# Cross network on one core: weight loads in another order and on other queues, the last tiles in another order, the last group's sums and stores moved

## The chip, the cores and the metric

The kernel runs on one core of a Trainium2 chip. The metric is device microseconds (us) of one execution, the median over several. The core has five engines, each with its own instruction queue in program order: PE (TensorE, matmuls), DVE (VectorE), ACT (ScalarE), POOL (GpSimd) and SP (SyncE), which here only issues DMAs. ACT can issue DMAs too, on a queue of its own. Engines and DMAs wait for each other by semaphores.

## The reference

A deep-and-cross network: six layers, each a 416 x 416 projection of x with a bias, multiplied element by element by x0 and added to x.

```python
B, F, D, L = 16384, 26, 16, 6
Din = min(F * D, 1024)          # 416
...
x = x0
for l in range(L):
    proj = jnp.einsum('bd,de->be', x, ws[l]) + bs[l]
    x = x0 * proj + x
return x
```

All inputs and the output are bf16.

## The kernel before

**Layout.** The 16384 rows are cut into 8 groups of 2048 rows. A group is held transposed (features on partitions, rows along the free dimension), in 4 chunks of 512 rows (`j`, 0 to 3). The 416 features are three blocks of 128 (`t` or `i`, 0 to 2) and a tail of 32. The tails of the four chunks lie under each other on 128 partitions (`x3s`, and the last 512 columns of `x0s`). The weights of a layer are `wm[l]` (the first 384 input features), `w3[l]` (the last 32, repeated four times under each other, one copy for each chunk) and `wbd[l]` (the 32 x 32 corner, block-diagonal, which POOL copies out of `w3` in `make_wbd`).

**Tiles.** A tile (g, l, i) is output block i of layer l of group g: 12 matmuls of 128 x 512 (`full`, L402) and 4 that use 32 rows of the array, side by side (`rows32`, L414), into four PSUM banks. ACT adds the bias and moves the tile to SBUF (`evacuate`, L361), DVE multiplies by x0 (L370) and adds x (L375). The tails of several jobs are computed together (`tails`, L427 and L432, then L388, L390, L392). Mostly two tiles are paired: the first runs `full` and then `rows32`, the second `rows32` and then `full`.

**Order.** A list `order` walks the 48 jobs (g, l) along diagonals, so that several groups are in flight and PE does not wait for the job before it. In that list the tile (6, 5, 2), the third block of the last layer of group 6, is taken out and put at the end (L550, L551), behind the three tiles of (7, 4). Job (7, 5), the last layer of the last group, is not in the list; it is done by the code from L657 on. For job (7, 4) and for (0, 0) the third block is evacuated chunk by chunk (`fine_after`, `step = 1`).

**A small scheduler.** Every instruction is recorded with `add`, with the names it reads and writes. `Program` derives the waits and writes out one queue for each engine. Each queue keeps the order of the `add` calls, but for DVE: an instruction with `hold` is put behind the next one with `release`, so that the sum of a piece stands after the product of the next piece. A DMA belongs to a `lane`, a semaphore of its own; a reader of one DMA of a batch waits for the whole batch of its lane. At the end SP waits for every lane (L162, L179).

**The start.** Group 0 is loaded row-major in four pieces of 512 rows (L457, SP's queue, 416 KB each) and transposed by PE (`transposed_chunk`, L483 and L488; ACT evacuates blocks 0 and 1, L493, DVE the rest, L496 and L499). Twenty-eight matmuls on the identity (L469) come first. The biases (L459) and layer 0's weights (`load_w(0, "act")`, L279 and L281) go over ACT's queue, layer 1's over SP's. PE then does chunk 0, the biases, chunk 1, the first three matmuls of tile (0, 0, 0), chunk 2, three more, chunk 3, and the rest. The other groups are loaded by transposing DMAs on SP (`load_group`, L295 to L302), with the weights of later layers among them (`W_LOAD`).

**The output of groups 0 to 6** (`output`, L520): three transposing DMAs for the three blocks (L524), four for the tails (L529), into one staging tile `ost`, and one store of 1664 KB (L535), all on SP. It is recorded once a group's last tile and its tails are done.

**The last stage, job (7, 5)**, is computed row-major, so that its output needs no transpose. The rows of each chunk are taken in four residues, blocks `kk` of 0 to 3. For each kk and chunk j, `nat_full` (L700) and `nat_rows` (L711, L716) make the projection with the bias; `nat_mul` copies it to SBUF on ACT (L728) and multiplies by x0 on DVE (L730; the very last directly from PSUM, L725); `nat_add` adds x (L735). `to_rows` turns x of two blocks at a time to row-major on PE (L675, L682), evacuated half by ACT (L692), half by DVE (L695). `nat_store` (L740) stores a block of 416 KB, the last one in two halves. Four banks `bka` and four banks `bkb` are used in turn.

Of the kernel before, what the change touches and what calls it, by code (L numbers as in the profile page):

```python
# [3 lines left out]
P = 128  # L4
CH = 512
T32 = 32
# [15 lines left out]
class Program:  # L22
# [125 lines left out]
    def emit(self):  # L148
        nc = self.nc
        self.flush()  # L150
        self._solve()
        sems = {e: nc.alloc_semaphore(f"sem_{e}") for e in self.ENGINES if e != "sp"}
        for lane in self.lanes:
            sems[lane] = nc.alloc_semaphore(f"sem_{lane}")
        count = {}
        for e, ops in self.queue.items():
            n = 0
            for op in ops:
                if op.need and op.lane is None:
                    n += 1  # L160
                count[id(op)] = n
        ends = [(lane, 16 * sum(len(ops) for _, ops in b)) for lane, b in self.lanes.items()]  # L162

        def run(e, handle):
            for op in self.queue[e]:
                for dom, val, d in op.waits:
                    handle.wait_ge(sems[dom], val if d.lane is not None else count[id(d)])
                ins = op.fn(handle)
                if op.lane is not None:
                    ins.then_inc(sems[op.lane], 16)  # L170
                elif op.need:
                    ins.then_inc(sems[e], 1)

        with nc.Block("main") as block:

            @block.sync
            def _(h):
                run("sp", h)
                for lane, n in ends:  # L179
                    h.wait_ge(sems[lane], n)  # L180

            @block.gpsimd
            def _(h):
                run("pool", h)

            @block.scalar
            def _(h):
                run("act", h)

            @block.tensor  # L190
            def _(h):
                run("pe", h)

            @block.vector
            def _(h):
                run("dve", h)


def bass_standalone__cross_network_dcn__recsys_kernel(
# [75 lines left out]
        return got  # L275


    def load_w(l, eng):
        add(eng, lambda h: h.dma_start(wm[l][:, :, :], ws[l, 0:NT * P, :].rearrange("(t p) f -> p t f", p=P)),  # L279
            writes=[("wm", l)], lane=f"w{l}", batch=0)  # L280
        add(eng, lambda h: h.dma_start(w3[l][:, :], ws[l, NT * P:D, :].unsqueeze(0).broadcast_to([NJ, T32, D])),  # L281
            writes=[("w3", l)], lane=f"w{l}", batch=0)

    def make_wbd(l):
        add("pool", lambda h: h.memset(wbd[l][:, :], 0.0), writes=[("wbd", l)])
        for j in range(NJ):
            q = slice(j * T32, (j + 1) * T32)
            add("pool", lambda h, q=q: h.tensor_copy(wbd[l][q, q], w3[l][q, NT * P:D]),  # L288
                reads=[("w3", l)], writes=[("wbd", l)])

    def load_group(g):
        s = slot(g)
# [116 lines left out]
    def rows32(g, l, i, banks, first):  # L409
        src, stok = x3_src(g, l)  # L410
        ecols = slice(i * P, (i + 1) * P)
        for j in range(NJ):
            q = slice(j * T32, (j + 1) * T32)
            add("pe", lambda h, q=q, j=j: h.matmul(  # L414
                bank(banks[j]), w3[l][q, ecols], src[q, :], start=first, stop=not first,
                tile_position=(j * T32, 0)),
                reads=stok + [("w3", l)], writes=[("ps", banks[j])])

    def tails(batch):
        bs_ = take(len(batch))  # L420
# [32 lines left out]
        return ap[j * CH:(j + 1) * CH, :].rearrange("(p k) f -> p k f", k=KK)  # L453

    g0 = x0[0:GC, :]
    for j in range(NJ):
        add("sp", lambda h, j=j: h.dma_start(x0n[:, j, :, :], perm(g0, j)),  # L457
            writes=[("nat", j)], lane=f"nat{j}", batch=0)
    add("act", lambda h: h.dma_start(bs_sb[0:L, :], bs[:, :]), writes=["bs_sb"], lane="bs", batch=0)  # L459
    load_w(0, "act")  # L460
    make_wbd(0)
    load_w(1, "sp")
    load_group(1)
    load_w(2, "sp")
    make_wbd(1)
    make_wbd(2)

# [7 lines left out]
    def transposed_chunk(j):  # L475
        ba, bb = (0, 1) if j % 2 == 0 else (2, 3)
        s = slot(0)
        for t in range(NT + 1):
            b, o = (ba, t * CH) if t < 2 else (bb, (t - 2) * CH)
            for k in range(KK):  # L480
                c = slice(o + k * P, o + (k + 1) * P)
                if t < NT:
                    add("pe", lambda h, t=t, k=k, b=b, c=c: h.transpose(  # L483
                        psum_t(b)[:, c], x0n[:, j, k, t * P:(t + 1) * P], ident[:, :]),
                        reads=[("nat", j), x0_tok(nat, 0, 0), "ident"], writes=[("ps", b)])
                else:
                    q = slice(j * T32, (j + 1) * T32)
                    add("pe", lambda h, k=k, b=b, c=c, q=q: h.matmul(  # L488
                        psum_t(b)[q, c], x0n[:, j, k, NT * P:D], ident[:, :], is_transpose=True,
                        tile_position=(0, j * T32)),  # L490
                        reads=[("nat", j), x0_tok(nat, 0, 0), "ident"], writes=[("ps", b)])
        for t in range(2):
            add("act", lambda h, t=t: h.activation(  # L493
                x0s[s][:, cols(t, j)], psum_t(ba)[:, t * CH:(t + 1) * CH], ACT_F.Copy),
                reads=[("ps", ba)], writes=[x0_tok(s, t, j)])
        add("dve", lambda h: h.tensor_copy(x0s[s][:, cols(2, j)], psum_t(bb)[:, 0:CH]),  # L496
            reads=[("ps", bb)], writes=[x0_tok(s, 2, j)])
        q = slice(j * T32, (j + 1) * T32)
        add("dve", lambda h: h.tensor_copy(x0s[s][q, XW:XW + CH], psum_t(bb)[q, CH:2 * CH]),  # L499
            reads=[("ps", bb)], writes=[("x03q", s, j)])  # L500
# [19 lines left out]
    def output(g):  # L520

        s, s3 = xset[(g, L)], xtail[(g, L)]
        for t in range(NT):
            add("sp", lambda h, t=t: h.dma_start_transpose(  # L524
                ost[:, :, t * P:(t + 1) * P], xs[s][:, t * GC:(t + 1) * GC]),
                reads=[("x", s, t, j) for j in range(NJ)], writes=[("ost", t)], lane="ot", batch=g)
        for j in range(NJ):
            q = slice(j * T32, (j + 1) * T32)
            add("sp", lambda h, j=j, q=q: h.dma_start_transpose(  # L529
                ost[:, j * KK:(j + 1) * KK, NT * P:D], x3s[s3][q, :]),  # L530
                reads=[("x3", s3)], writes=[("ost", NT, j)], lane="ot", batch=g)
        rows = out[g * GC:(g + 1) * GC, :]
        pat = "(j p k) f -> p j k f" if g == 0 else "(j k p) f -> p j k f"
        kw = dict(j=NJ, k=KK)
        add("sp", lambda h: h.dma_start(  # L535
            rows.rearrange(pat, **kw), ost[:, :, :].rearrange("p (j k) f -> p j k f", j=NJ)),
            reads=[("ost", t) for t in range(NT)] + [("ost", NT, j) for j in range(NJ)],
            writes=[("out", g)], lane="out", batch=g)
        free_x.append(s)
        free_3.append(s3)  # L540
# [7 lines left out]
            if (jb, i) in where:  # L548
                items.append(("tails", where[(jb, i)]))
    late = items.index(("tile", (LAST - 1, L - 1), NT - 1))  # L550
    items.append(items.pop(late))  # L551


    single = 0
# [18 lines left out]
    def start_job(g, l):  # L573
        started.add((g, l))
        xset[(g, l + 1)] = free_x.pop(0)
        if (g, l) in W_LOAD:
            load_w(W_LOAD[(g, l)], "sp")
            make_wbd(W_LOAD[(g, l)])
        if (g, l) in G_LOAD:
            load_group(G_LOAD[(g, l)])  # L580
# [124 lines left out]
    def nat_rows(kk, bks, first):  # L705
        for part in range(2):
            for j in range(NJ):
                q = slice(j * T32, (j + 1) * T32)
                st, sp_ = first and part == 0, not first and part == 1
                if part == 0:  # L710
                    add("pe", lambda h, j=j, q=q, st=st: h.matmul(  # L711
                        bank(bks[j], n=D), x3col(j, kk), w3[l][q, :], start=st, stop=False,
                        tile_position=(j * T32, 0)),
                        reads=tok3 + [("w3", l)], writes=[("ps", bks[j])])
                else:
                    add("pe", lambda h, j=j, sp_=sp_: h.matmul(  # L716
                        bank(bks[j], n=D), ones[j * T32:j * T32 + 1, :], brow[j * T32:j * T32 + 1, :],
# [17 lines left out]
        add("dve", lambda h: h.tensor_tensor(o, o, x5v, ALU.add),  # L735
            reads=[("on", j, kk), ("x5n", j, kk // 2)], writes=[("on", j, kk)])

    def nat_store(kk, j0, j1, lane):
        dst = out[LAST * GC:B, :].rearrange("(j p k) f -> p j k f", j=NJ, k=KK)[:, j0:j1, kk, :]
        add("sp", lambda h: h.dma_start(dst, on[:, j0:j1, kk, :]),  # L740
            reads=[("on", j, kk) for j in range(j0, j1)], writes=[("out7", kk, j0)], lane=lane, batch=0)

    bka, bkb = take(NJ), take(NJ)
# [6 lines left out]
    for j in range(NJ):  # L750
        nat_full(1, j, bkb[j], False)
        nat_mul(1, j, bkb[j])
    to_rows(0, bka)
    for kk in range(2):
        for j in range(NJ):
            nat_add(kk, j)
        nat_store(kk, 0, NJ, f"o7_{kk}")
    nat_rows(2, bkb, True)
    for j in range(NJ):
        nat_full(2, j, bkb[j], False)  # L760
        nat_mul(2, j, bkb[j])
    to_rows(1, bka)
    for j in range(NJ):
        nat_add(2, j)
    nat_store(2, 0, NJ, "o7_2")
    nat_rows(3, bkb, True)
    for j in range(NJ):
        nat_full(3, j, bkb[j], False)
        nat_mul(3, j, bkb[j])
        nat_add(3, j)  # L770
        if j % 2 == 1:
            nat_store(3, j - 1, j + 1, f"o7_3_{j}")

    pr.emit()

# [27 lines left out]
```

## Time and profile before

| what | value |
|---|---|
| median of 6 runs | 498.66 us (497.05 to 500.68) |
| the profiled execution | 498.28 us, of which 496.5 us are its span |
| PE busy | 478.5 us (96%) |
| DVE busy | 405.5 us (82%) |
| ACT busy | 342.7 us (69%) |
| POOL busy | 9.5 us (2%) |
| mean granted clock of PE | 0.989 |
| DMA | 47.65 MB, mean 96 GB/s |

The span runs from the first to the last instruction. Where a time is given without more, it is counted from the span's start. In the profile, a line of an engine's timeline has the start, the duration over all its instructions, the engine, the line of the kernel, the operation with what it writes and reads, how many, and in brackets the idle time before it and what ended it. SPq and ACTq are DMA issues on these queues. The granted clock is the share of full speed that PE was given.

The largest waits of the profile, in all:

| who waited | for | us |
|---|---|---|
| ACT, L361 | PE, L414 | 106.6 |
| DVE, L370 | ACT, L361 | 68.1 |
| POOL, L288 | DMA of the weights | 39.8 |
| ACT, L361 | PE, L402 | 23.5 |
| DVE, L496 | PE, L488 | 12.8 |
| PE, L402 | DMA of the weights | 3.0 |

### The profile page before, as it was taken

Reading aid. Unit: us, or ns where it says so; the run is one execution under the profiler, and the core shown is the slowest. Engines: PE = TensorE matmul, PEld = TensorE weight load, DVE = VectorE, ACT = ScalarE, POOL = GpSimd, SP = SyncE. Lnnn points to the kernel's source line nnn. Section 1 sums busy time; section 2 is a strip of 40 time slices with the busy share of each in tenths; the row PEclk is TensorE's granted clock in tenths of the full one; section 3 lists DMA queues with packets and bytes.
Section 4 is the critical chain, followed back from the end, with each engine's and each line's share of the span. In section 5 each row is a group of like instructions: output and inputs, shape, how many; then the busy total and the mean of one; then the engine's idle time right before and its main releaser. Section 6 shows DMA issues by size and latency. Waiting matters only on the chain.

```text
span 496.5 us, 8094 instructions
## 1 busy us (share of the span) xinstructions
PE 478.5 (96%) x3251; PEld 203.2 (41%) x3251; DVE 405.5 (82%) x710; ACT 342.7 (69%) x371; POOL 9.5 (2%) x37
## 2 busy tenths in 40 slices
PE   6999999999999999999999999999999999999990
PEld 5433444444444444434444444444444444444460
DVE  1578888888888888888888888888888888888892
ACT  3667767677677777667677767767667767777680
POOL 2002100000000000000000000000000000000000
PEclk9999999999999999999999999999999999999997
DMA  9797880000001694347516944560000452334428
GB/s 247 148 197 138 154 179 5 1 1 0 2 1 26 111 241 80 50 87 193 129 33 106 245 73 72 130 214 1 1 1 1 79 106 93 61 76 141 85 55 275
DMA packets 127185, 47.65 MB, mean 96 GB/s; under 512 B 107298, under 2 KB 125612, under 8 KB 127148
## 3 DMA queue, kind: packets, MB, share of 16 engines
q1 hardware_dynamic: 126604, 46.71, 42.8%
q8 instruction: 25, 0.41, 0.4%
q10 hardware_dynamic: 544, 0.43, 0.3%
q14 instruction: 12, 0.10, 0.1%
HBM read 5.97 MB, written 13.63 MB: 39 GB/s over the span
## 4 chain that ended last, share of the span: by engine, by line
PE 92%; DVE 3%; DMA 2%; ACT 1%; issue 0%; ACTq 0%
PE ps L402 74%; PE ps L414 8%; PE ps L427 6%; PE ps L432 2%; DMA w<-in_ws_dram 2%; DVE x L735 1%; PE ps L700 1%; DVE x L375 1%; ACT tw L361 1%; DVE tw L370 1%; PE ps L483 0%; DVE x L695 0%; DVE x L730 0%; PE ps L675 0%; PE ps L488 0%
## 5 line engine op out<-in xcount | busy, mean ns | idle before, releaser
L361 ACT ACTIVATE tw<-ps,bias 128x1024 bf16<-128x1024 f32 (+1 forms) x295 | 300.4, 1073 | 130.0 <-PE ps L414 106.6
L402 PE MATMUL ps<-x,wm 128*128 128x512 bf16 x1692 | 380.5, 380 | 3.9 <-DMA w<-in_ws_dram 3.0
L370 DVE TENSOR_TENSOR tw<-tw,x 128x1024 bf16<-128x1024 bf16 (+1 forms) x286 | 194.2, 683 | 68.7 <-ACT tw L361 68.1
L402 PEld LDWEIGHTS ps<-x,wm 128*128 128x128 bf16 x1692 | 159.0, 98 | 218.8 <-issue 31.6
L375 DVE TENSOR_TENSOR x<-tw,x 128x1024 bf16<-128x1024 bf16 (+1 forms) x286 | 182.0, 677 | 0.0
L414 PE MATMUL ps<-x,w 32*128 32x512 bf16 x564 | 44.5, 380 | 0.4 <-DVE x L392 0.4
L427 PE MATMUL ps<-x,wm 128*32 128x512 bf16 x564 | 38.7, 380 | 0.0
L388 ACT ACTIVATE ts<-ps,bias 128x512 bf16<-128x512 f32 x47 | 28.7, 699 | 0.0
L414 PEld LDWEIGHTS ps<-x,w 32*128 32x128 bf16 x564 | 9.0, 92 | 33.5 <-issue 32.4
L427 PEld LDWEIGHTS ps<-x,wm 128*32 128x32 bf16 x564 | 13.8, 96 | 15.5 <-issue 3.2
L392 DVE TENSOR_TENSOR x<-ts,x 128x512 bf16<-128x512 bf16 x47 | 18.6, 417 | 0.0
L390 DVE TENSOR_TENSOR ts<-ts,x 128x512 bf16<-128x512 bf16 x47 | 18.5, 417 | 0.0
L432 PE MATMUL ps<-x,wbd 128*32 128x512 bf16 x188 | 18.3, 379 | 0.0
L496 DVE COPY x<-ps 128x512 bf16<-128x512 bf16 x4 | 1.7, 424 | 12.8 <-PE ps L488 12.8
L493 ACT ACTIVATE x<-ps 128x512 bf16<-128x512 bf16 x8 | 4.3, 594 | 7.5 <-PE ps L483 7.5
L700 PE MATMUL ps<-wm,x 128*128 128x416 bf16 x48 | 9.2, 341 | 0.0
L288 POOL COPY wbd<-w 32x32 bf16<-32x32 bf16 x24 | 7.4, 307 | 41.0 <-DMA w<-in_ws_dram 39.8
L432 PEld LDWEIGHTS ps<-x,wbd 128*32 128x32 bf16 x188 | 5.0, 97 | 5.1
L728 ACT ACTIVATE x<-ps 128x416 bf16<-128x416 f32 x15 | 6.5, 545 | 0.5 <-PE ps L716 0.5
L700 PEld LDWEIGHTS ps<-wm,x 128*128 128x128 bf16 x48 | 5.1, 115 | 3.8 <-issue 1.3
L735 DVE TENSOR_TENSOR x<-x,x 128x416 bf16<-128x416 bf16 x16 | 5.1, 371 | 0.1
L730 DVE TENSOR_TENSOR x<-x,x 128x416 bf16<-128x416 bf16 x15 | 4.8, 369 | 0.0
(32 smaller groups left out, 38.9 us busy)
## 6 DMA issues: line engine op xcount, KB each, us to landing
out_dram<-ost SPq DMA_DIRECT2D x7, 1664.0 KB, 6.8
x<-in_x_dram SPq DMA_DIRECT2D x8, 416.0 KB, 6.4
wm<-in_ws_dram SPq DMA_DIRECT2D x5, 312.0 KB
out_dram<-x SPq DMA_DIRECT2D x3, 416.0 KB, 6.9
x<-Tb SPq DMA_DIRECT2D x28, 32.0 KB, 1.9
ost<-x SPq DMA_TRANSPOSE x49, 3.0
w<-in_ws_dram SPq DMA_DIRECT2D x5, 104.0 KB
out_dram<-x SPq DMA_DIRECT2D x2, 208.0 KB, 5.7
```

The costliest lines, as they stand in the source:

```text
L361: add("act", lambda h, a=a, w=w, b0=b0: h.activation(tw[r][:, a * CH:(a + w) * CH], psum[:, b0 * CH:(b0 + w) * CH], ACT_F.Identity, bias=b ...
L370: add("dve", lambda h, a=a, e=e: h.tensor_tensor(tw[r][:, a * CH:e * CH], tw[r][:, a * CH:e * CH], x0s[s0][:, i * GC + a * CH:i * GC + e * ...
L375: add("dve", lambda h, a=a, e=e: h.tensor_tensor(xs[so][:, i * GC + a * CH:i * GC + e * CH], tw[r][:, a * CH:e * CH], src(i, a, e), ALU.ad ...
L388: add("act", lambda h: h.activation(ts[r][:, :], bank(b), ACT_F.Identity, bias=bias[:, 3, l:l + 1], scale=1.0), reads=[("ps", b), "bias"], ...
L390: add("dve", lambda h: h.tensor_tensor(ts[r][:, :], ts[r][:, :], x0s[s0][:, XW:XW + CH], ALU.mult), reads=[("ts", r)] + x03_toks(s0), writ ...
L392: add("dve", lambda h: h.tensor_tensor(x3s[so][:, :], ts[r][:, :], src, ALU.add), reads=[("ts", r)] + stok, writes=[("x3", so)], hold=True)
L402: add("pe", lambda h, t=t, j=j: h.matmul(bank(banks[j]), wm[l][:, t, ecols], src(t, j, j + 1), start=(first and t == 0), stop=(not first a ...
L414: add("pe", lambda h, q=q, j=j: h.matmul(bank(banks[j]), w3[l][q, ecols], src[q, :], start=first, stop=not first, tile_position=(j * T32, 0)),
L427: add("pe", lambda h, t=t, j=j, src=src, l=l, b=b: h.matmul(bank(b, j * T32, (j + 1) * T32), wm[l][:, t, NT * P:D], src(t, j, j + 1), star ...
L432: add("pe", lambda h, j=j, s3=s3, l=l, b=b: h.matmul(bank(b, j * T32, (j + 1) * T32), wbd[l][:, j * T32:(j + 1) * T32], s3, start=False, s ...
L700: add("pe", lambda h, t=t: h.matmul(bank(b, n=D), xcol(t, j, kk), wm[l][:, t, :], start=(first and t == 0), stop=(not first and t == NT - 1)),
L735: add("dve", lambda h: h.tensor_tensor(o, o, x5v, ALU.add), reads=[("on", j, kk), ("x5n", j, kk // 2)], writes=[("on", j, kk)])
```

## The change

1. **Weights.** `load_w` becomes `load_wm` and `load_w3`, each with a lane of its own. `w3` is loaded by four DMAs of 32 rows instead of one that repeats the rows; its readers depend on their copy (one lane, so they wait for all four).
2. **Load order at the start.** The first row-major piece is loaded in two halves (two of its four row residues each), each with its lane. Layer 0's `wm` follows on SP's queue, then the other three pieces, then layer 1's `wm`. The `w3` of layers 0 and 1 go over ACT's queue, eight DMAs behind the biases. From layer 2 on both parts are on SP's.
3. **Output of groups 0 to 6.** The transposing DMA of block 2 comes after those of the tails.
4. **Tile order.** (6, 5, 2) is put before the last tile instead of behind it: (7, 4, 1), (6, 5, 2), (7, 4, 2). With that (7, 4, 2), which was the second of a pair with its chunks evacuated between its matmuls, stands alone: all its matmuls, `rows32`, then the four evacuations.
5. **Last stage.** The second `to_rows` goes to before the sums of blocks 0 and 1, with banks `bkb`; block 2 takes `bka`, its `nat_rows` before those sums. In blocks 2 and 3 each sum comes one product later. The last half of the last store is issued on ACT's queue.
6. **End.** SP waits for the lanes of the output only.

```diff
-        ends = [(lane, 16 * sum(len(ops) for _, ops in b)) for lane, b in self.lanes.items()]
+        ends = [(lane, 16 * sum(len(ops) for _, ops in b)) for lane, b in self.lanes.items() if lane.startswith("out")]
...
-    def load_w(l, eng):
+    def load_wm(l, eng):
         add(eng, lambda h: h.dma_start(wm[l][:, :, :], ws[l, 0:NT * P, :].rearrange("(t p) f -> p t f", p=P)),
-            writes=[("wm", l)], lane=f"w{l}", batch=0)
-        add(eng, lambda h: h.dma_start(w3[l][:, :], ws[l, NT * P:D, :].unsqueeze(0).broadcast_to([NJ, T32, D])),
-            writes=[("w3", l)], lane=f"w{l}", batch=0)
+            writes=[("wm", l)], lane=f"wm{l}", batch=0)
+
+    def load_w3(l, eng):
+        for j in range(NJ):
+            add(eng, lambda h, j=j: h.dma_start(w3[l][j * T32:(j + 1) * T32, :], ws[l, NT * P:D, :]),
+                writes=[("w3", l, j)], lane=f"w3{l}", batch=0)
...
-    for j in range(NJ):
-        add("sp", lambda h, j=j: h.dma_start(x0n[:, j, :, :], perm(g0, j)),
-            writes=[("nat", j)], lane=f"nat{j}", batch=0)
+    def load_nat(j, k0, k1):
+        add("sp", lambda h: h.dma_start(x0n[:, j, k0:k1, :], perm(g0, j)[:, k0:k1, :]),
+            writes=[("nat", j, k) for k in range(k0, k1)], lane=f"nat{j}{k0}", batch=0)
+
     add("act", lambda h: h.dma_start(bs_sb[0:L, :], bs[:, :]), writes=["bs_sb"], lane="bs", batch=0)
-    load_w(0, "act")
+    load_nat(0, 0, 2)
+    load_nat(0, 2, KK)
+    load_wm(0, "sp")
+    load_w3(0, "act")
     make_wbd(0)
-    load_w(1, "sp")
+    for j in range(1, NJ):
+        load_nat(j, 0, KK)
+    load_wm(1, "sp")
+    load_w3(1, "act")
     load_group(1)
-    load_w(2, "sp")
+    load_wm(2, "sp")
+    load_w3(2, "sp")
...
-        for t in range(NT):
-            add("sp", lambda h, t=t: h.dma_start_transpose(
+        def turn(t):
+            add("sp", lambda h: h.dma_start_transpose(
...
+        turn(0)
+        turn(1)
         for j in range(NJ):
...
+        turn(2)
...
-    items.append(items.pop(late))
+    items.insert(len(items) - 2, items.pop(late))
...
-    def nat_store(kk, j0, j1, lane):
+    def nat_store(kk, j0, j1, lane, eng="sp"):
...
     to_rows(0, bka)
+    to_rows(1, bkb)
+    nat_rows(2, bka, True)
     for kk in range(2):
         for j in range(NJ):
             nat_add(kk, j)
-        nat_store(kk, 0, NJ, f"o7_{kk}")
-    nat_rows(2, bkb, True)
+        nat_store(kk, 0, NJ, f"out7_{kk}")
     for j in range(NJ):
-        nat_full(2, j, bkb[j], False)
-        nat_mul(2, j, bkb[j])
-    to_rows(1, bka)
-    for j in range(NJ):
-        nat_add(2, j)
-    nat_store(2, 0, NJ, "o7_2")
+        nat_full(2, j, bka[j], False)
+        nat_mul(2, j, bka[j])
+        if j:
+            nat_add(2, j - 1)
+    nat_add(2, NJ - 1)
+    nat_store(2, 0, NJ, "out7_2")
     nat_rows(3, bkb, True)
     for j in range(NJ):
         nat_full(3, j, bkb[j], False)
         nat_mul(3, j, bkb[j])
-        nat_add(3, j)
-        if j % 2 == 1:
-            nat_store(3, j - 1, j + 1, f"o7_3_{j}")
+        if j:
+            nat_add(3, j - 1)
+        if j == 2:
+            nat_store(3, 0, 2, "out7_3")
+    nat_add(3, NJ - 1)
+    nat_store(3, 2, NJ, "out7_4", "act")
```

## The prediction

> **What bounds the kernel now.** I read the busy shares first: TensorE (PE) is busy 478.5 of 496.5 us, so only about 18 us can be won without removing matmuls. The waits say where they lie: 1.8 us before the identity exists, 3.0 us for the first weights, about 1 us at 25 us; the rest, 12 us, is the stretch after PE's last matmul (484.5 us). The middle is a solid PE stream that the change does not touch. So I read two timelines, the first 17 us and the last 40. The head (start, duration, engine, line):
>
> ```profile
> 1.36 0.41 ACTq L279 DMA_DIRECT2D wm<-in_ws_dram  x1
> 1.80 0.65 ACTq L281 DMA_DIRECT2D w<-in_ws_dram  x1
> 2.48 1.28 ACT L493 ACT_TABLE_LOAD   x1 [2.48 <-issue]
> ...
> 6.06 0.84 PE L483 MATMUL ps<-ident,x 128*128 128x128 bf16 x12
> ...
> 10.19 0.81 PE L402 MATMUL ps<-x,wm 128*128 128x512 bf16 x3 [2.96 <-DMA w<-in_ws_dram]
> ...
> 13.48 1.49 PE L483 MATMUL ps<-ident,x 128*128 128x128 bf16 x12
> ...
> 16.63 0.39 PE L414 MATMUL ps<-x,w 32*128 32x512 bf16 x4
> ```
>
> Layer 0's weights are asked for at 1.36 and 1.80 us and are there at 10.19: PE stands for 3 us. The same twelve transposes take 0.84 us at 6.06 and 1.49 us at 13.48, and the table of windows says why (stretch, length, PE, weight loads, DVE, ACT, POOL, granted clock, DMA share, GB/s):
>
> ```profile
> 8.00:10.00 2.00, 0.00 (x0) 0.00 (x0) 0.14 (x1) 0.00 (x0) 0.00 (x0) 1.00 1.82 211
> 10.00:12.00 2.00, 1.81 (x19) 1.29 (x19) 0.00 (x0) 0.52 (x2) 1.42 (x7) 0.86 0.77 175
> 12.00:14.00 2.00, 2.00 (x11) 0.98 (x10) 0.85 (x2) 0.57 (x2) 0.61 (x3) 0.50 1.28 146
> 14.00:16.00 2.00, 2.00 (x18) 1.33 (x16) 0.64 (x2) 1.08 (x2) 0.00 (x0) 0.78 1.07 232
> ```
>
> The 3 us gap is paid twice: the clock falls to 0.50 some 4 us after it began. The end:
>
> ```profile
> 475.17 2.58 SPq L524 DMA_TRANSPOSE ost<-x  x1
> ...
> 477.79 5.09 SPq L529 DMA_TRANSPOSE ost<-x  x4
> ...
> 484.01 0.37 SPq L535 DMA_DIRECT2D out_dram<-ost  x1
> 484.43 7.58 SPq L740 DMA_DIRECT2D out_dram<-x  x5
> ...
> 487.20 0.37 DVE L735 TENSOR_TENSOR x<-x,x 128x416 bf16<-128x416 bf16 x1
> ```
>
> The chain names DVE last (487.6 us), yet the span ends at 496.5. Windows from 486 to 494 show 309 to 339 GB/s: group 6's store (1664 KB) and group 7's (1664 KB) run through the DMA engines one after the other, 3.4 MB at 0.33 MB/us = 10.3 us from about 486. **The start of group 6's store, 484.01, sets the end.** It waits for SP, which held group 6's third transpose until tile (6,5,2), last on PE, was through DVE at 475.15, and only then issued the four tail transposes (5.1 us), whose data had been ready since 465.9.
>
> **Head, step by step.** Before, the weights went over ACT's queue beside 3.3 KB rows of x on SP's queue, and came 8.3 us after issue. Now wm of layer 0 stands third on SP's queue, behind 416 KB. The first x piece landed 3.2 us after 0.73, so at 3.9; at 340 GB/s (windows 2 to 8 us: 334 to 379) wm is there at 4.9, x piece 1 at 6.1 to 6.4, piece 2 at 7.6, piece 3 at 8.8. None comes late, and the weights stop being the wait. Next late is **ACT**: its queue now holds bs and eight w3 issues ahead of the table load and the first evacuation (before: three). One issue step is unknown: nearest rows are ACT's own 0.44 (wm) and 0.68 (w3 of 128 rows), and SP's 32-row copies at L302, median 0.59. I take 0.58: 1.36 + 8 x 0.58 = 6.0, table load to 7.3, two evacuations of 0.55 to 8.4. PE's first chunk needs them: matmuls 7.9 to 8.85, the third transposed chunk at 8.85 instead of 10.84. From there at full clock, each chunk 1.2 us of transposes and 0.65 of matmuls, rows of layer 0 start at 13.2 instead of 16.6: **-3.4 us**. At a step of 0.44 PE waits for x piece 1 only (-4.2); at 0.68 it is -2.6.
>
> Two rules of the Trainium skill speak against this. "ScalarE: Activation LUTs", section What ACT_TABLE_LOAD costs, adds a drain of 1.38 us to a load of 1.28. The row has 1.28, then 1.58 us idle that end with PE's transposes, so a drain could hide there; by the page the head gives -2.0. I follow the row, since nothing is in flight on ACT at its first load, and keep the page's value for the range. "DMA: Bandwidth & Descriptors", section Issuing engines are not separate DMA queues, says that queues share 16 engines, and issuing from a second one saves sequencer time alone; by it moving w3 saves nothing. The row (8.3 us for 416 KB at 1.36, while the first 416 KB of x needed 3.2) shows that the queue's neighbours did matter; here what helps is that wm moves ahead of x pieces 1 to 3.
>
> At nothing: w3 as four copies moves the same bytes; layer 0's are needed at 13 us. Layers 2 to 5 cost SP three more issues each, 3 x 0.6 = 1.8 us a layer, ahead of x loads. Group 1's last piece landed near 24.9 and is needed at 34.3 (30.9 now), group 2's near 41.7 and at 58.9 (55.5), group 3's near 63.5 and at 88.9 (85.5); behind all four layers, 7.2 us, 14 us of cover stay. POOL's copies to wbd start sooner. Splitting x piece 0 adds one issue of 0.45 us on SP ahead of later pieces; PE is in its 28 warm matmuls until 4.8. The shorter list of end waits is nothing: those waits are passed while the last store is in flight. Turning column block 2 after the tails in groups 0 to 5 moves SP only; PE waits for no such DMA in the middle.
>
> **Tail, step by step** (times of before; the head's shift moves all alike). Tile (6,5,2) now runs on PE at 465 to 468, (7,4,2) last. DVE is through the former at 471.75 instead of 475.15, and the four tail transposes go out from 465.9 to 471.0, ahead of it. Third transpose 471.75, landing 4.6 later (median at L524): group 6's store starts at 476.4, not 484.0, and is done at 483.2 (6.8 to landing). It no longer collides with group 7, and the bound is PE and DVE:
>
> 1. **New stall.** The last stage's first matmuls (L700) need the third block of (7,4,2), which is now evacuated right before: rows end at 471.0, ACT 471.1 to 471.8 (0.69 at 128x512), DVE's products for chunks 0 and 1, then its first sum at 473.15. PE stands at 471.4 to 473.2, and is through the first four chunks at 475.3 instead of 473.2: **+2.05 on PE**.
> 2. ACT copies eight blocks (3.4 us) from 475.8; DVE's eight products end at 479.55 instead of 477.5. Transposes of blocks 0, 1: PE to 479.9.
> 3. The second to_rows now stands before the sums of blocks 0 and 1: PE 1.6 us, to 481.5. DVE, which takes its four copies in order, ends them at 482.65 (before: two at 478.97), then eight sums 2.4 us: stores 0 and 1 at about 483.8 and 485.
> 4. Block 2: eight operations of 0.30, to 487.4. Block 3, sums now one product behind: seven of 0.30 and one of 0.51, to **490.1** (before 487.6; pairs cost 0.69 each there, 0.6 here).
> 5. Last store, 208 KB, on ACT's queue. Landing is not shown free of backlog: below by 1.6 (the large store's 6.8 less 1664 KB at 330 GB/s) plus 0.65, so 2.3; above by 5.3, the least at L740, under backlog. Its issue may take 1.35 us, as at L740, instead of 0.4. I take 3.0. The span ends at 493.2, not 496.5: **-3.2** (with 2.3: -4.0; with 5.3: -1.0).
>
> A falling clock in the new 1.8 us stall could cost PE up to 1.7 us (half of the 3.4 us at about half clock that followed the 3 us gap); stalls of 0.3 to 0.4 us near 26 us left it at 1.00. "TensorE: Matmul & The Clock Gate", section What's actually happening, has the clock fall only after an idle window of about 3.4 us; the row fell after 3.0. I take nothing, and keep the 1.7.
>
> **Sum.** -3.4 - 3.2 = -6.6. The profiled execution took 498.28 us (span 496.5 and 1.8 around it): 491.7. The median of runs is 0.38 higher, so I name **492.1 us**. Its own range: best -4.2 - 4.0 = 490.4; worst -2.0 - 1.0 = 495.6.
>
> **Rivals.**
> - *Tail given back:* store latency under some backlog, a clock dip and the stall together leave the tail at 0, head -3.4: 495.3. For: the only store rows are 5.3 to 7.6 us, and DVE ends later than before. Against: after 483 there are gaps between stores, so no backlog is in sight. Chance 0.15.
> - *Head kept by ACT or by a slow wm:* tail -3.2 alone, 495.5. For: eight issues on an in-order engine. Against: the 0.44 to 0.68 steps. Chance 0.07.
> - *Slower:* each of ACT's eight w3 issues takes as long as an issue does[...]; L740's take 1.35 to 2.0 us, L302's longest was 1.77. At 1.8 us a step: 8 x (1.8 - 0.58) = +9.8 over my head, which becomes +6.4; with the tail -3.2 the total is +3.2, 501.9. It decides from a step of 1.4 us on. Against: ACT's own issues in the same microseconds took 0.41 to 0.65. Chance 0.04.
> - *The change does not act:* group 6's store stays late since SP is held elsewhere in 459 to 475. SP's lines there show only these transposes, waiting for DVE. It would be about 495, and is in the second's number.
>
> Forecast: 0.74. A change of 0.5%, 2.5 us, is what this kernel's measurement can tell from none. The first two rivals lie at -3.2 to -3.4, near it, so some of their 0.22 falls to no change: 0.73 + 0.14 faster by more, 0.09 the same, 0.04 slower. Range 489.6 to 495.7: from the best end with 0.8 for what I may have missed, to the rivals.
>
> **What would show it.** Right: the first L402 matmul near 8 us instead of 10.2 with clock 1.00 to 16 us, rows of layer 0 near 13; table load at about 6; group 6's store near 473 (476.4 less the head's 3.4); a PE wait of about 1.8 us for DVE at the first L700 matmuls; DVE's last sum near 486.7 and the span's end some 3 us behind it. Wrong: a first ACT evacuation after 10 us; stores still back to back at 330 GB/s at the end; a clock of 0.5 in the last stage; PE waits in the middle.

## The result, and the profile after

The changed kernel takes **493.29 us** (median of 15 runs, 491.25 to 498.15), the kernel before 498.72 us beside it (34 runs). The ratio is 0.9904, with a 95% interval of 0.9884 to 0.9924: about 4.8 us, 1%, faster. The profiled executions went from 498.28 to 493.29 us, their spans from 496.5 to 491.5. In a later series the same kernel took 494.90 us (7 runs) beside 498.24, a ratio of 0.9930 (0.9907 to 0.9954); both intervals stand below 1.

The head of the changed kernel, from its timeline (line numbers are those of the changed file: L494 transposes, L405 is `full`, L417 `rows32`, L504 the first evacuations):

```profile
1.35 4.91 ACTq L284 DMA_DIRECT2D w<-in_ws_dram  x8
...
6.29 1.28 ACT L504 ACT_TABLE_LOAD   x1 [6.29 <-issue]
...
7.58 1.08 ACT L504 ACTIVATE x<-ps 128x512 bf16<-128x512 bf16 x2
...
8.22 0.84 PE L494 MATMUL ps<-ident,x 128*128 128x128 bf16 x12 [1.16 <-DMA x<-in_x_dram]
...
9.32 0.82 PE L405 MATMUL ps<-x,wm 128*128 128x512 bf16 x3
...
11.73 0.83 PE L494 MATMUL ps<-ident,x 128*128 128x128 bf16 x12
...
14.23 0.40 PE L417 MATMUL ps<-x,w 32*128 32x512 bf16 x4
```

Layer 0's weights are waited for no more. PE waits for x instead: the second transposed chunk starts at 8.22, released by the DMA of x piece 1, with 1.16 us of idle time. From there all runs at full speed (0.83 at 11.73, where it was 1.49 at 13.48), and rows of layer 0 start at 14.23, 2.4 us earlier.

The end, from the same kernel's timeline (L543 and L535 transpose the output, L550 is group 6's store, L716 `nat_full`, L744 ACT's copies, L756 the last group's stores):

```profile
463.15 5.00 SPq L543 DMA_TRANSPOSE ost<-x  x4
...
469.34 2.00 SPq L535 DMA_TRANSPOSE ost<-x  x1
...
470.78 3.29 PE L716 MATMUL ps<-wm,x 128*128 128x416 bf16 x10 [1.73 <-DVE x L378]
...
473.61 0.37 SPq L550 DMA_DIRECT2D out_dram<-ost  x1
...
474.91 3.38 ACT L744 ACTIVATE x<-ps 128x416 bf16<-128x416 f32 x8 [3.82 <-PE ps L732]
...
483.00 5.22 SPq L756 DMA_DIRECT2D out_dram<-x  x4
...
488.25 0.65 DVE L751 TENSOR_TENSOR x<-x,x 128x416 bf16<-128x416 bf16 x2
488.93 0.42 ACTq L756 DMA_DIRECT2D out_dram<-x  x1
```

Group 6's store starts at 473.61 instead of 484.01. In its place stands PE's stall of 1.73 us at the first `nat_full`, and the matmuls behind it run at half speed for a while, as the windows of this kernel show (columns as before: PE, weight loads, DVE, ACT, POOL, granted clock, DMA share, GB/s):

```profile
470.00:472.00 2.00, 1.22 (x5) 0.56 (x6) 2.00 (x7) 1.09 (x2) 0.00 (x0) 0.86 0.81 156
472.00:474.00 2.00, 2.00 (x7) 0.59 (x6) 0.40 (x2) 0.00 (x0) 0.00 (x0) 0.50 0.56 107
474.00:476.00 2.00, 2.00 (x22) 0.98 (x22) 0.51 (x2) 1.09 (x3) 0.00 (x0) 0.78 0.71 233
...
480.00:482.00 2.00, 2.00 (x31) 1.19 (x29) 1.45 (x4) 1.98 (x3) 0.00 (x0) 1.00 0.04 10
482.00:484.00 2.00, 2.00 (x18) 0.95 (x17) 2.00 (x8) 2.00 (x5) 0.00 (x0) 1.00 0.04 14
```

At 480 to 484 the DMA engines are all but idle between group 6's store and the last group's. In the kernel before, PE and DVE were through by 487.6, and the stores still ran back to back behind them:

```profile
488.00:490.00 2.00, 0.00 (x0) 0.00 (x0) 0.00 (x0) 0.00 (x0) 0.00 (x0) 0.83 1.03 328
490.00:492.00 2.00, 0.00 (x0) 0.00 (x0) 0.00 (x0) 0.00 (x0) 0.00 (x0) 0.50 1.05 339
```

So DMA no longer bounds the end; PE's stage, and DVE's chain behind it, do. DVE is through at 488.9, and the span ends 2.6 us later.

### The profile page after: what moved, and what is told of

Same layout as the page of the kernel before. It is cut to its first block, busy times and chain, and to the rows that moved or that the text cites. A ratio compares the mean times of both kernels' runs of the same rounds, so it can differ in the third digit from the quotient of the medians.

```text
span 491.5 us, 8102 instructions
## 1 busy us (share of the span) xinstructions
PE 480.3 (98%) x3251; PEld 203.3 (41%) x3251; DVE 405.7 (83%) x710; ACT 343.4 (70%) x372; POOL 10.3 (2%) x37
## 4 chain that ended last, share of the span: by engine, by line
PE 93%; DVE 3%; DMA 1%; ACT 1%; issue 0%; SPq 0%; DVEq 0%
PE ps L405 75%; PE ps L417 8%; PE ps L430 6%; PE ps L435 2%; DMA x<-in_x_dram 1%; PE ps L716 1%; DVE x L751 1%; ACT tw L364 1%; DVE x L378 1%; DVE tw L373 1%; PE ps L691 1%; PE ps L494 0%; DVE x L746 0%; PE ps L499 0%; SPq L460 0%
## 5 line engine op out<-in xcount | busy, mean ns | idle before, releaser
L405 PE MATMUL ps<-x,wm 128*128 128x512 bf16 x1692 | 379.8, 380 | 1.0 <-DVE x L378 1.0
L405 PEld LDWEIGHTS ps<-x,wm 128*128 128x128 bf16 x1692 | 158.9, 98 | 215.6 <-issue 28.2
L417 PE MATMUL ps<-x,w 32*128 32x512 bf16 x564 | 44.5, 380 | 0.3 <-DVE x L395 0.3
L417 PEld LDWEIGHTS ps<-x,w 32*128 32x128 bf16 x564 | 9.0, 92 | 33.5 <-issue 32.4
L430 PEld LDWEIGHTS ps<-x,wm 128*32 128x32 bf16 x564 | 13.8, 96 | 15.5 <-issue 3.2
L716 PE MATMUL ps<-wm,x 128*128 128x416 bf16 x48 | 10.7, 372 | 1.7 <-DVE x L378 1.7
L744 ACT ACTIVATE x<-ps 128x416 bf16<-128x416 f32 x15 | 6.8, 536 | 4.5 <-PE ps L732 3.8
L746 DVE TENSOR_TENSOR x<-x,x 128x416 bf16<-128x416 bf16 x15 | 5.4, 373 | 3.3 <-ACT x L744 3.1
L716 PEld LDWEIGHTS ps<-wm,x 128*128 128x128 bf16 x48 | 5.1, 119 | 6.7 <-DVE x L378 2.7
L504 ACT ACTIVATE x<-ps 128x512 bf16<-128x512 bf16 x8 | 4.3, 594 | 1.5 <-PE ps L494 1.3
```

The source lines that it names most:

```text
L405: add("pe", lambda h, t=t, j=j: h.matmul(bank(banks[j]), wm[l][:, t, ecols], src(t, j, j + 1), start=(first and t == 0), stop=(not first a ...
L417: add("pe", lambda h, q=q, j=j: h.matmul(bank(banks[j]), w3[l][q, ecols], src[q, :], start=first, stop=not first, tile_position=(j * T32, 0)),
L430: add("pe", lambda h, t=t, j=j, src=src, l=l, b=b: h.matmul(bank(b, j * T32, (j + 1) * T32), wm[l][:, t, NT * P:D], src(t, j, j + 1), star ...
L716: add("pe", lambda h, t=t: h.matmul(bank(b, n=D), xcol(t, j, kk), wm[l][:, t, :], start=(first and t == 0), stop=(not first and t == NT - 1)),
```

## The experiments

All ran against the kernel before, in three series of four kernels (`h_only` to `turn_only`, `fill` to `last_sp`, `turn_head` to `after_again`), each series on one chip; a difference between series is less sure than one within. "Head" is the start of layer 0's rows in the profiled execution, "tail" the time from there to the span's end, so that the head's gains and losses drop out of it. Both are of one execution for each kernel.

| kernel | median us (before beside it) | ratio, 95% interval | head | tail |
|---|---|---|---|---|
| before | 498.66 | 1 | 16.6 | 479.9 |
| changed | 493.29 (498.72) | 0.9904, 0.9884 to 0.9924 | 14.2 | 477.3 |
| h_only | 496.02 (498.64) | 0.9946, 0.9926 to 0.9967 | 15.6 | 479.7 |
| t_only | 495.62 (498.64) | 0.9933, 0.9909 to 0.9957 | 17.6 | 477.3 |
| order_turn | 495.64 (498.64) | 0.9926, 0.9902 to 0.9950 | 18.4 | 475.7 |
| turn_only | 493.89 (498.64) | 0.9902, 0.9869 to 0.9935 | 17.3 | 475.6 |
| fill | 492.56 (498.46) | 0.9885, 0.9855 to 0.9916 | 15.5 | 475.3 |
| x1_first | 491.75 (498.46) | 0.9876, 0.9849 to 0.9903 | 14.0 | 475.8 |
| w3_one | 494.24 (498.46) | 0.9939, 0.9915 to 0.9963 | 15.8 | 475.8 |
| last_sp | 491.77 (498.46) | 0.9885, 0.9858 to 0.9912 | 13.6 | 479.1 |
| turn_head | 492.09 (498.24) | 0.9872, 0.9849 to 0.9896 | 13.7 | 475.5 |
| both_a | 488.78 (498.24) | 0.9810, 0.9788 to 0.9831 | 13.7 | 473.8 |
| both_b | 488.48 (498.24) | 0.9806, 0.9785 to 0.9827 | 12.7 | 473.8 |
| after_again | 494.90 (498.24) | 0.9930, 0.9907 to 0.9954 | 15.7 | 478.9 |

### Which part gains

`h_only` is the kernel before with parts 1 and 2. `t_only` is the kernel before with parts 3, 4 and 5. `order_turn` has parts 3 and 4, `turn_only` part 3 alone:

```diff
# turn_only
-        for t in range(NT):
-            add("sp", lambda h, t=t: h.dma_start_transpose(
+        def turn(t):
+            add("sp", lambda h: h.dma_start_transpose(
...
+        turn(0)
+        turn(1)
...
+        turn(2)
# order_turn: the same, and
-    items.append(items.pop(late))
+    items.insert(len(items) - 2, items.pop(late))
```

> The kernel before with the weights' lanes and the load order of the start alone (parts 1 and 2); the end is as before. Theory A, two gains that add: rows of layer 0 start at 14.2 us instead of 16.6, the end is the old one, so -2.4 us (ratio 0.995). Rival B, the gain comes from the end alone: the head's gain is lost later, 0 us.

> The kernel before with the parts at the end alone (output order, tile order, last stage; 3, 4 and 5). Theory A: -2.6 us (ratio 0.995), group 6's store near 476, PE stall of 1.7 us before the last stage's third block and a clock of 0.5 after it. Rival B: the whole -5 us. Rival C, the gain comes from the start alone: 0 us.

> As t_only, but with the last stage of the kernel before (parts 3 and 4 only). Theory A, the gain of the end is group 6's earlier store, and the moved sums and the split last store are worth little: within 0.8 us of t_only. Rival: the new last stage is what gains; then this is 2 us or more slower than t_only.

> The kernel before with the third transposing DMA behind the tails' alone (part 3). Theory A: the third transpose still goes out at 475.2, lands 4.4 later, and group 6's store starts at 479.6 instead of 484.0; the two stores still run back to back, so the end comes 4.4 us earlier: -4.4 us, more than all three parts of the end together, since (7,4,2) keeps its cover and PE does not stall. Rival: the tile order is needed for any gain; then 0 to -1 us.

`h_only` gave -2.6 us and `t_only` -3.0 on the medians: two gains that add, theory A. Which of parts 1 and 2 brings the head's share was not tried by itself; the runs of the head below say something on it. `order_turn` equals `t_only` in the median, so the new last stage brings nothing that these runs can show. **`turn_only` gave -4.75 us**, as theory A had it: one transposing DMA put behind four others is worth as much as the whole change (0.9902 against 0.9904). Its timeline (L524 transposes block 2, L539 group 6's store, L744 the last group's):

```profile
475.83 2.61 SPq L524 DMA_TRANSPOSE ost<-x  x1
...
480.35 0.37 SPq L539 DMA_DIRECT2D out_dram<-ost  x1
480.85 7.80 SPq L744 DMA_DIRECT2D out_dram<-x  x5
...
487.87 0.38 DVE L739 TENSOR_TENSOR x<-x,x 128x416 bf16<-128x416 bf16 x1
```

and its windows:

```profile
484.00:486.00 2.00, 1.20 (x7) 0.56 (x5) 1.97 (x8) 1.48 (x4) 0.00 (x0) 1.00 1.04 331
486.00:488.00 2.00, 0.00 (x0) 0.00 (x0) 1.90 (x6) 0.00 (x0) 0.00 (x0) 1.00 1.06 339
488.00:490.00 2.00, 0.00 (x0) 0.00 (x0) 0.24 (x1) 0.00 (x0) 0.00 (x0) 0.98 1.04 315
```

The last block still goes out when tile (6, 5, 2) is done, and the store starts 4.5 us after it, where before the four tail transposes stood between (475.17 to 484.01, 8.8 us). The stores still run back to back at 315 to 339 GB/s, and DVE is done 4.7 us ahead of the span's end: here DMA is the bound, with no stall on PE. `turn_head` adds the start's parts to it:

> The changed kernel with the tile order and the last stage of the kernel before (parts 4 and 5 undone): the start's parts and the third transposing DMA behind the tails'. Theory A, the tile order and the new last stage bring nothing beside the moved DMA, and pay for an earlier store with PE's stall: 491.5 us, 1 to 2 us faster than the changed kernel. Rival: with the head earlier the later stores bind, and parts 4 and 5 are needed: as the changed kernel or 1 us slower.

Its store starts 3.7 us earlier than `turn_only`'s, as its head does (3.6), and DMA binds its end in the same way:

```profile
476.64 0.37 SPq L550 DMA_DIRECT2D out_dram<-ost  x1
...
482.00:484.00 2.00, 0.00 (x0) 0.00 (x0) 1.93 (x6) 0.00 (x0) 0.00 (x0) 1.00 1.04 335
484.00:486.00 2.00, 0.00 (x0) 0.00 (x0) 0.62 (x2) 0.00 (x0) 0.00 (x0) 1.00 1.05 325
```

It took 492.09 us, and the changed kernel beside it (`after_again`) 494.90; the two intervals, 0.9849 to 0.9896 and 0.9907 to 0.9954, do not meet. (It also has the end waits of the kernel before; part 6 was not tried alone.) Against the changed kernel's first series, 0.9884 to 0.9924, the intervals do overlap, as those of `turn_only` and `t_only` do. So no run shows a gain of the tile order and the new last stage beside part 3; they cost 1.7 us (`t_only` against `turn_only`, not clear of the scatter) to 2.8 us (`after_again` against `turn_head`, clear of it).

### The stall and the clock

`fill` changes only the first block of the last stage: its 32-row parts and biases, and blocks t = 0, 1 of all four chunks, come before any block 2.

```diff
-    for j in range(NJ):
-        nat_full(0, j, bka[j], True)
-    nat_rows(0, bka, False)
+    nat_rows(0, bka, True)
+    for ts_ in ((0, 1), (2,)):
+        for j in range(NJ):
+            nat_full(0, j, bka[j], False, ts_)
```

> The changed kernel, but the first block of the last stage does its tail rows and biases and the blocks t = 0, 1 of all four chunks before any t = 2: 2.1 us of PE work stand in the stall. Theory A, the stall and the half clock after it delay the whole last stage by 3 us and DVE's chain with it: DVE ends 3 us earlier, -2.5 to -3 us against the changed kernel (489.5 to 490.8 us), clock 1.00 from 470 to 484. Rival, DVE or the stores bound the end anyway: within 0.8 us of the changed kernel.

> The changed kernel itself, beside the three others on one chip. Both theories: 493.3 us within 1 us; PE's stall of 1.7 us before the last stage in the profile again, with or without a fall of the clock after it, which decides between some 491.5 and 493 to 495 us.

`fill` shows three waits of 0.30 to 0.32 us where 1.73 stood, a clock of 1.00 through its last stage, and a tail of 475.3 instead of 477.3:

```profile
472.69 0.37 PE L716 MATMUL ps<-wm,x 128*128 128x416 bf16 x1 [0.31 <-DVE x L378]
```

Its head was slow in the profile (15.5). The median is 0.7 us below the changed kernel's, the intervals overlap, and theory A's 2.5 to 3 us did not come: the number is the rival's. Counted from the head, DVE's last sum ends 2.0 us sooner than in the changed kernel, where theory A had 3. So the gain is shown in the tail of one execution, 2 us against an execution with the fall of the clock, but only 0.5 against `x1_first`, which had the stall and no fall.

Whether the clock falls weighs more than the stall itself. Seven profiled executions have the same stall of 1.73 us. In three of them (`order_turn`, `x1_first`, `w3_one`) the clock stays at 1.00; the windows of `order_turn`:

```profile
474.00:476.00 2.00, 1.05 (x5) 0.52 (x6) 1.86 (x6) 1.26 (x3) 0.00 (x0) 1.00 0.70 136
476.00:478.00 2.00, 2.00 (x23) 0.77 (x22) 0.57 (x2) 0.30 (x1) 0.00 (x0) 1.00 0.67 126
```

In four it falls, here `after_again`:

```profile
472.00:474.00 2.00, 1.74 (x8) 0.74 (x9) 1.88 (x6) 0.57 (x1) 0.00 (x0) 0.85 1.11 212
474.00:476.00 2.00, 2.00 (x16) 0.68 (x18) 0.00 (x0) 0.00 (x0) 0.00 (x0) 0.50 0.27 50
476.00:478.00 2.00, 2.00 (x13) 0.59 (x6) 1.32 (x4) 1.86 (x5) 0.00 (x0) 0.50 0.97 318
478.00:480.00 2.00, 2.00 (x7) 0.88 (x6) 0.93 (x3) 0.95 (x3) 0.00 (x0) 0.50 1.03 332
480.00:482.00 2.00, 2.00 (x33) 1.66 (x33) 0.75 (x2) 1.00 (x2) 0.00 (x0) 0.94 0.64 205
```

The time at half clock, worked out as what is missing to 1.00 in each window, times 2 us, over 0.50, is 3.4 us in the changed kernel and `t_only`, 6.8 in `after_again` and `last_sp`. The tails follow: 475.7 to 475.8 without a fall, 477.3 with 3.4 us of it, 478.9 to 479.1 with 6.8. (The median of `after_again`, 494.90, lies 0.6 us outside what was expected of it, and within what was named for a fall of the clock.) The changed kernel's 15 runs say the same by their mean clock: the two at 1.000 took 491.25 and 491.50 us, the four at 0.989 and 0.990 took 494.56 to 497.08. So much of its spread goes with the clock. The mean is a rough sign, for it also counts a fall behind the last matmul, which costs nothing (about 3 us at half clock from 488.5 on in the changed kernel's profile); and the one slowest run, 498.15 us at 0.993, is not explained by it. Where the clock falls, it does so 2.4 to 3.1 us after the stall began (worked out from the windows), when PE is at work again.

### The head

`x1_first` puts x piece 1 ahead of layer 0's `wm`. `w3_one` loads `w3` with one repeating DMA again, on the changed queues. `last_sp` issues the last store on SP.

```diff
# x1_first
+    load_nat(1, 0, KK)
     load_wm(0, "sp")
...
-    for j in range(1, NJ):
+    for j in range(2, NJ):
         load_nat(j, 0, KK)
# w3_one
-        for j in range(NJ):
-            add(eng, lambda h, j=j: h.dma_start(w3[l][j * T32:(j + 1) * T32, :], ws[l, NT * P:D, :]),
-                writes=[("w3", l, j)], lane=f"w3{l}", batch=0)
+        add(eng, lambda h: h.dma_start(w3[l][:, :], ws[l, NT * P:D, :].unsqueeze(0).broadcast_to([NJ, T32, D])),
+            writes=[("w3", l, j) for j in range(NJ)], lane=f"w3{l}", batch=0)
# last_sp
-    nat_store(3, 2, NJ, "out7_4", "act")
+    nat_store(3, 2, NJ, "out7_4")
```

> The changed kernel with x piece 1 ahead of layer 0's wm on SP's queue. Theory A, PE waits at 7.06 to 8.22 for x piece 1 and then for nothing: piece 1 is there near 7, the first L405 matmul is then held by ACT's evacuation at 8.1 (its end 8.66 for the second block), so about -0.7 us. Rival, the issues on ACT hold the head: 0 us. Second rival, wm is then late in its turn: first L405 matmul after 9.3, slower by up to 1 us.

> The changed kernel with w3 of each layer as one repeating DMA again (same queues). ACT issues three DMAs instead of nine before its table load, which then starts near 2.5 us instead of 6.3. Theory A, x piece 1 is what PE waits for and w3's small transfers do not matter to it: first L405 matmul still near 9.3, within 0.3 us of the changed kernel. Rival 1, ACT holds the head: -1.2 us. Rival 2, w3's copies slow the x pieces on the 16 engines: piece 1 near 6.3, -1.5 us or more.

> The changed kernel with the last half store on SP's queue again. SP is done with the store before at 488.2, and the last one's data come at 488.9. Theory A, the second queue is worth nothing: within 0.3 us of the changed kernel. Rival: the split saves an issue and a queue behind it, 0.7 us or more slower without it.

`w3_one` tells the two suspects of the head apart. Its timeline (L503 evacuates, L493 transposes, L404 is `full`):

```profile
5.30 1.08 ACT L503 ACTIVATE x<-ps 128x512 bf16<-128x512 bf16 x2 [1.38 <-PE ps L493]
...
8.48 1.46 PE L493 MATMUL ps<-ident,x 128*128 128x128 bf16 x12 [2.40 <-DMA x<-in_x_dram]
...
10.81 0.86 PE L404 MATMUL ps<-x,wm 128*128 128x512 bf16 x2 [0.33 <-ACT x L503]
```

ACT is ready at 5.30, 2.3 us earlier than in the changed kernel, and it helps nothing: PE waits 2.40 us for x piece 1, and then runs at half clock (0.50 in the window 8 to 10 us). Its first `full` is 1.5 us later than the changed kernel's, where theory A had no change. So x piece 1, not ACT's issues, holds the head of the changed kernel, and the four copies are not what delays that piece. They may even help: the ratio of 0.9939 (0.9915 to 0.9963) is above that of `last_sp` in the same series (0.9858 to 0.9912), which differs from the changed kernel only in the queue of the last store. Here piece 1 was issued at 2.47 and landed at 8.5, against 2.14 and 8.1 in the changed kernel; why `w3_one` is slower was not tried further.

In `x1_first` the piece is there 0.85 us sooner (7.37), and PE's first `full` is then held by ACT:

```profile
6.83 1.28 ACT L505 ACT_TABLE_LOAD   x1 [6.83 <-issue]
...
8.13 1.09 ACT L505 ACTIVATE x<-ps 128x512 bf16<-128x512 bf16 x2
...
9.27 0.60 PE L405 MATMUL ps<-x,wm 128*128 128x512 bf16 x2 [0.72 <-ACT x L505]
```

That matmul starts only 0.05 us sooner than in the changed kernel: theory A's 0.7 did not come, and the first rival's cause, ACT's issues, is the next wait as soon as piece 1 is early. Rows start at 13.96, 0.3 us sooner in one execution, less than the head's own scatter, and the median of 491.75 does not stand clear of the changed kernel's interval.

That the head scatters is seen in six executions of the changed start (changed, `h_only`, `fill`, `last_sp`, `turn_head`, `after_again`): 13.6 to 15.7 us, mean 14.7. Four of the old start have 16.6 to 18.4, mean 17.5. The scatter has a pattern: where PE waited 1.23 us or less for piece 1, the clock stayed at 1.00 and rows started by 14.2; where it waited 1.49 us or more, the clock fell and rows started at 15.5 or later (eight executions, with `x1_first` and `w3_one`). The wait is not a free variable, though: it is longer where chunk 0 was transposed faster (0.99 us for its twelve transposes in `h_only`, 1.49 in the changed kernel).

`last_sp` has the stall with 6.8 us of half clock in its profile, and yet a median of 491.77, 1.5 us below the changed kernel's with intervals that overlap. The rival's loss of 0.7 us is not seen; theory A's 0.3 us is too fine for this scatter. No gain of the second queue for the last store is seen.

### A version that beats both

`both_a` and `both_b` start from the changed kernel and take out what the runs had shown: x piece 1 early, layer 1's `w3` off ACT's queue, the stall filled, and DVE's copies of the second `to_rows` behind the sums of blocks 0 and 1 (`to_rows` is split into its PE part, `rows_pe`, and its copies, `rows_out`).

```diff
+    nat_rows(0, bka, True)
     for j in range(NJ):
-        nat_full(0, j, bka[j], True)
-    nat_rows(0, bka, False)
+        nat_full(0, j, bka[j], False, (0, 1))
+    nat_rows(1, bkb, True)
     for j in range(NJ):
+        nat_full(0, j, bka[j], False, (2,))
         nat_mul(0, j, bka[j])
-    nat_rows(1, bkb, True)
+        nat_full(1, j, bkb[j], False, (0, 1))
     for j in range(NJ):
-        nat_full(1, j, bkb[j], False)
+        nat_full(1, j, bkb[j], False, (2,))
         nat_mul(1, j, bkb[j])
-    to_rows(0, bka)
-    to_rows(1, bkb)
+    rows_pe(0, bka)
+    rows_pe(1, bkb)
+    rows_out(0, bka)
...
         nat_store(kk, 0, NJ, f"out7_{kk}")
+    rows_out(1, bkb)
# both_b, the start: x piece 1 as ACT's first DMA
+    load_nat(1, 0, KK, "act")
     add("act", lambda h: h.dma_start(bs_sb[0:L, :], bs[:, :]), writes=["bs_sb"], lane="bs", batch=0)
```

> The changed kernel with x piece 1 ahead of layer 0's wm, layer 1's w3 on SP's queue, the stall filled with the blocks t = 0, 1 of the first two residues, and DVE's copies of the second to_rows behind the sums of blocks 0 and 1. Theory A: no stall over 0.4 us and clock 1.00 in the last stage; DVE's chain ends 3 us earlier than in the changed kernel and the start is 0.5 us earlier: 489 to 490 us. Rival: group 6's and group 7's stores, 3.4 MB at 330 GB/s from 474 on, bind first: 491 to 492 us.

> As both_a, with x piece 1 as the first DMA of ACT's queue instead of third on SP's. Theory A, pieces in one queue delay each other: piece 1 is there before 6.8 us, PE does not wait for it, the start is 0.7 us earlier than both_a's. Rival, all queues share the same 16 DMA engines and piece 1 comes no earlier, or piece 0 comes later: 0 to +1 us against both_a.

They took 488.78 and 488.48 us, 0.981 of the kernel before, and stayed within 1 us from run to run (4 and 5 runs). Four things were put together; how much each brings was not tried apart. The lines of `both_b` (L495 transposes, L719 is `nat_full`, L754 the sums):

```profile
6.69 0.84 PE L495 MATMUL ps<-ident,x 128*128 128x128 bf16 x12
...
8.02 0.59 PE L405 MATMUL ps<-x,wm 128*128 128x512 bf16 x2 [0.16 <-ACT x L505]
...
470.08 3.00 PE L719 MATMUL ps<-wm,x 128*128 128x416 bf16 x16
...
483.26 0.65 DVE L754 TENSOR_TENSOR x<-x,x 128x416 bf16<-128x416 bf16 x2
```

PE waits for neither x piece 1 nor a third block, and the clock is 1.00 to the last matmul. The tail is 473.8, 3.5 us shorter than the changed kernel's. x piece 1 landed at 4.8 in `both_b` and at 6.8 in `both_a`; some 0.9 of these 2 us are its earlier issue. In return the two halves of piece 0 took 3.9 and 4.2 us to land instead of 2.5 and 2.9 (0.26 us of waiting at 5.4). PE was ready for piece 1 only at 6.69, so a landing at 6.8 would have held it for 0.1 us. Between `both_a` and `both_b` the heads differ by 1.0 us in the profiles and the medians by 0.3, with intervals that overlap.

## Why the prediction was right, and where its sums were off

The forecast was 492.1 us from -3.4 at the head and -3.2 at the tail; the profiled execution has -2.4 and -2.6, and the medians of runs moved by 5.4. Group 6's store was what held the end, and layer 0's weights what held the head: there the mechanism was right. Two terms were mis-sized, x piece 1 at the head and the clock at the tail. The tail's own sum has a slip: 490.1 and 3.0 make 493.1, 3.4 us below 496.5, not 3.2. That the median came within 1.2 us is in part luck, since the same kernel gave 494.9 in the later series.

- **x piece 1 "at 6.1 to 6.4. None comes late."** It came at 8.2, 6.0 us after its issue, and was what the head waited for. Piece 0 was there at 4.0, as forecast (3.9); wm landed at 6.8 instead of 4.9, and pieces 2 and 3 at 9.5 and 10.7 instead of 7.6 and 8.8: all behind piece 0 came some 1.9 us late, in order and at the forecast's spacing. The step that failed is that a DMA is there as soon as its bytes and those ahead of it in the queue have moved at 340 GB/s: by 8 us some 1.9 MB had been moved (windows of the changed kernel: 285, 303 and 357 GB/s from 2 us on), more than the 1.2 MB that stood up to piece 1 in its queue and the few small copies beside it. So later pieces were under way while piece 1 was unfinished. Why a piece behind others completes so late was not tried further; `both_b` shows that it lands 2 us sooner than in `both_a` as the first DMA of another queue.
- **ACT as "next late".** Its own term held: an issue step of 0.61 us instead of 0.58, the table load at 6.29 instead of 6.0, the first evacuation at 7.58. It was hidden behind x piece 1, and comes out in `x1_first`. The drain of 1.38 us that the Trainium skill gives for a switch of tables ("ScalarE: Activation LUTs", section What ACT_TABLE_LOAD costs) does not appear at this first load: it ends at 7.57 and the first evacuation starts at 7.58. The row was the better guide.
- **Weights.** wm never made PE wait, and the second payment for the gap, the slow clock at 12 to 16 us, went with it. From the first `full` on, my times are matched: 4.9 us to the rows, where I had 5.3.
- **Group 6's store.** Forecast at 476.4 less the head's shift of 2.4, so 474.0; it was 473.6. Stores 0 and 1 find the DMA engines idle, as forecast. I counted the moved transpose and the tile order together. The moved transpose alone brings the store to 480.35 in `turn_only` (479.7 when its later head, 0.7 us, is taken off), and that is worth the whole gain; the 3.7 us more that the tile order brings buy nothing, since PE's stall and DVE's chain then bound the end.
- **New stall.** 1.8 us forecast, 1.73 measured.
- **The clock, "I take nothing, and keep the 1.7."** It cost 1.5: ACT's copies started at 474.9, where the sum with the shift has 473.4. I had weighed the idle window of about 3.4 us that the Trainium skill gives ("TensorE: Matmul & The Clock Gate", section What's actually happening) against a row of 3.0, and chose the page's side for 1.8. The runs put the bound lower: four of seven stalls of 1.73 us were enough. A clock of 0.50 in the last stage was one of my own signs of being wrong, and it came. DVE ended at 488.9, where the sum has 487.7.
- **Last store.** 3.0 taken, 2.6 measured. The issue takes 0.37 to 0.42 us without a backlog, so L740's 1.35 us were the queue in front of it: in `turn_only`, where the backlog is left, five issues take 7.8 us again.
- **Rivals.** ACT's slow issues were not seen (0.61 a step, against the 1.4 from which it decides). "Tail given back" was near: with 6.8 us of half clock, as in `after_again`, the tail is 478.9, and 1.0 us is all that is left of the tail's gain.

## What to carry to other kernels

Look in the in-order queue in front of the last large transfer for work that is ready but stands behind a wait: moving one DMA was worth the whole 1%, and no gain was seen from the reordering of tiles built around it. When a wait is removed, ask for each thing behind it when it arrives, not when it was asked for. And a stall on PE of 1.5 us or more can cost more than its length, since the clock may fall behind it: with the stall filled and the start's wait gone, `both_a` and `both_b` spread over less than 1 us (4 and 5 runs), where the changed kernel spread over 6.9 (15 runs) and, in their own series, over 4.2 (7 runs). Filling the stall alone (`fill`) left 4.4 (6 runs).

## What the runs showed of the hardware

- Half clock while PE works comes in pieces: 3.4 us at the start of the kernel before and in the last stage of the changed kernel and `t_only`, 6.8 in the last stage of `after_again` and `last_sp`. The window of about 3.4 us that the Trainium skill gives ("TensorE: Matmul & The Clock Gate", section What's actually happening) fits that length, but the idle time before a fall is shorter here: the clock fell after waits of 1.49 us and more at the start of the changed kernel and its variants (four executions), not after 1.23 and less (four), and after 1.73 in the last stage in four of seven.
- The Trainium skill ("DMA: Bandwidth & Descriptors", section Issuing engines are not separate DMA queues) says that a second issuing engine saves only the sequencer's time. For when one transfer lands, more moved here: x piece 1 landed 5.1 us after its issue as the third DMA of SP's queue (`both_a`) and 4.1 as the first of ACT's (`both_b`), while piece 0's halves took 1.3 to 1.4 us longer. That the queues share the engines, as the page says, fits the second number. For the last store, with nothing in front of it, no gain was seen.
